# Decoding float64 weights from one copy, with the sign moved by an activation, in an attention and two-layer gated network kernel

## The chip, the cores and the metric

The kernel runs on one core of one Trainium2 chip. The metric is the device time of one execution in microseconds (us). Three runs of the kernel before gave 648.14, 648.49 and 649.67 us, median 648.49 us. One more execution was profiled: it took 648.26 us, of which the trace spans 646.5 us from the first to the last instruction; 1.8 us lie around the span.

The engines are TensorE (PE; PEld is its weight load), VectorE (DVE), ScalarE (ACT), GpSimd (POOL) and SyncE (SP), which here only issues transfers. Each engine works through its own list of instructions in order.

## The reference

The weights `w_in`, `w_out` (first layer) and `w_gate`, `w_val`, `w_out` (second layer) arrive as float64; q, k and v are float32.

```python
k_sum = k.reshape(B, H, nb, block, D).max(axis=3)      # block = 32
v_sum = v.reshape(B, H, nb, block, D).mean(axis=3)
mask_l = np.abs(pos[:, None] - pos[None, :]) < window  # window = 16
scores_s = scale * einsum(q, k_sum) + np.log(block)
scores_all = concat([where(mask_l, scale * q @ k.T, -1e9), scores_s])
a = softmax(scores_all)                                # eps 1e-9 in the sum
x = a @ concat([v, v_sum])                             # 2 x 8 heads, 768 tokens, 64 wide
...
h = x @ w_in                                           # 1536 tokens, 512 -> 2048
x = (h / (1 + np.exp(-1.702 * h))) @ w_out             # 2048 -> 512
gate = 1 / (1 + np.exp(-(x @ w_gate)))                 # 512 -> 1536
return (gate * (x @ w_val)) @ w_out2                   # 1536 -> 512
```

## The kernel before, in words

**Attention.** There are 24 units: two batches, three groups of four query blocks, four pairs of heads. For each unit PE adds a mask and forms the scores (`ps_s`, L560 and L562), DVE takes the negative row maximum (`nm`, L567), ACT the exponentials with their sums (`e`, L575), DVE and POOL normalise (`rs` L582, `rr` L584, `e` L589), PE transposes (`ps_p`, L595), DVE copies (`pt`, L600), PE multiplies by the values (`ps_x`, L610), and the result is split into a rounded part `xH` (ACT, L628) and the rest `xL` (DVE, L631). POOL scales the keys (`kx`, L551), DVE takes maxima of keys (`ks`, L540) and sums of values (`vm`, L523).

**Layers.** Every large product is three matmuls in fp32r on high and low parts (L359 and L131). The first layer works on groups of 256 columns of its 2048 hidden columns and blocks of 512 tokens: `first` forms `ps_h`, gates it (ACT L383, DVE L374, ACT L375, POOL L376), and `second` multiplies by `w_out` into `ps_o`, which DVE adds to `acc` (L439). The first four of these steps are woven into the attention loop as a filler for PE. The second layer does two of its three token blocks with seven products instead of eight, from sums of weight blocks and of token blocks (`combine`, `token_sums`, `pair`).

**Weights.** There are 34 pieces of 128x1024 float64 elements, 1024 KB each. `fetch` issues two transfers for each piece: `raw` (L172), the words as they lie, and `mid` (L174), the same bytes shifted by 16 bits. Both have one buffer; the second piece goes to the buffers of `xH` and `xL` instead. `decode` makes a high part and a low part from them in six DVE and two ACT instructions, all on 128x1024 elements: the upper words as float32 are clamped (L104) and scaled on ACT (L105); the bits of the low part are cut out of `mid` (L108); the upper word is shifted left by 3 and masked (L110), the sign is put back (L112), ACT casts that to fp32r as the high part (L115); the exponent is cut out (L117), and bits times exponent times a constant is the low part (L119). `load` and `load_group` run these steps, one at each `yield`, and fetch the next piece after the first step; `pull(n)` takes n steps at a point of the loop.

**Order.** Transfers on SP stand in the order in which the program writes them. On the other engines the kernel is built with a scheduler that orders instructions by its own estimate of times, so the order of `pull` calls is only one of its inputs. In an engine's list an instruction that waits holds all behind it.

Of the kernel before, what the change touches and what calls it, by code (L numbers as in the profile page):

```python
# [8 lines left out]
F32 = mybir.dt.float32  # L9
F32R = mybir.dt.float32r  # L10
U32 = mybir.dt.uint32
U16 = mybir.dt.uint16
BF16 = mybir.dt.bfloat16
AF = mybir.ActivationFunctionType
ALU = mybir.AluOpType
# [14 lines left out]
def attention_moe_moe2_kernel(ctx: ExitStack, tc: tile.TileContext, ins: dict, out: bass.AP):  # L30
# [23 lines left out]

    const = ctx.enter_context(tc.tile_pool(name="const", bufs=1))
    xp = ctx.enter_context(tc.tile_pool(name="xp", bufs=NTB))
    wraw = ctx.enter_context(tc.tile_pool(name="wraw", bufs=1))
    wtmp = ctx.enter_context(tc.tile_pool(name="wtmp", bufs=1))

    ident = const.tile([P, P], F32, name="ident")  # L60
# [28 lines left out]
    acc_a = ctx.enter_context(tc.tile_pool(name="acc_a", bufs=1))  # L89
    ps_h = ctx.enter_context(tc.tile_pool(name="ps_h", bufs=2, space=PSUM))  # L90

    def decode(raw, mid, hi_out, lo_out):

        n = raw.shape[1] // 2
        head = raw.rearrange("p (n t) -> p n t", t=2)[:, :, 1]
        tail = mid.rearrange("p (n t) -> p n t", t=2)[:, :, 0]
        a, b, c = (wtmp.tile([P, n], U32, tag=f"d{x}", name=f"d{x}") for x in "abc")  # L100
        af, cf = a.bitcast(F32), c.bitcast(F32)
        ts = nc.vector.tensor_scalar

        ts(out=af, in0=head.bitcast(F32), scalar1=F64_MAX, scalar2=-F64_MAX, op0=ALU.min, op1=ALU.max)  # L104
        nc.scalar.activation(af, af, AF.Copy, scale=REBIAS)  # L105
        yield

        ts(out=b, in0=tail, scalar1=0x01FFFFFF, scalar2=None, op0=ALU.bitwise_and)  # L108
        yield
        ts(out=c, in0=a, scalar1=3, scalar2=0x7FFFF000, op0=ALU.logical_shift_left, op1=ALU.bitwise_and)  # L110
        yield
        nc.vector.scalar_tensor_tensor(  # L112
            out=c, in0=a, scalar=0x80000000, in1=c, op0=ALU.bitwise_and, op1=ALU.bitwise_or
        )
# [43 lines left out]
    for layer, g, i in wanted:  # L158
        w = mats[layer][i]
        last = i == len(mats[layer]) - 1  # L160
        src = [rows_of(x, g) if last else cols_of(x, g, n) for x, n in ((w.bitcast(U32), 2), (w.bitcast(U16), 4))]
        pieces.append((f"{layer}_{g}_{i}", *src))

    def fetch():

        if pieces:
            name, src, shifted = pieces.pop(0)
            n, m = src.shape[1], src.shape[2]

            homes = ((xp, "xH"), (xp, "xL")) if name == "1_0_1" else ((wraw, "raw"), (wraw, "mid"))  # L170
            raw, mid = (p.tile([P, n * m], U32, tag=t, name=f"{t}{name}") for p, t in homes)
# [3 lines left out]
            raws.append((raw, mid, (P, n, m // 2)))  # L175

    def load(slots, layer, g, i):
        raw, mid, shape = raws.pop(0)
        hi, lo = (slots.tile(list(shape), F32R, name=f"w{layer}_{g}_{i}{x}") for x in "HL")
        parts = decode(raw, mid, hi.rearrange("p a n -> p (a n)"), lo.rearrange("p a n -> p (a n)"))  # L180
# [283 lines left out]
    with tc.manual_schedule(engines={mybir.EngineType.SP}), ExitStack() as es:  # L464
# [236 lines left out]
        for t in range(-1, NU + LD):  # L701
            now[0] = t

            u = t + 2
            if u < NU and units[u][1] == 0:
                prep_k(units[u][0], units[u][2])
            for part, lag in ORDER:
                if 0 <= t - lag < NU:
                    part(t - lag)
            if 0 <= t < NU - 5:  # L710
                load_q(t + 5, nc.sync)
            if t == -1:
                sum_v(0, 0)
                sum_v(0, 1)
            if t == 0:
                sum_v(0, 2)
                sum_v(0, 3)
                sum_lay(0)
                load_v(0, 1)
                put_v(0, 0)  # L720
                put_v(0, 1)
            if t in (6, 7, 8, 9):
                sum_load(1, t - 6)
            if t in (7, 8, 9, 10):
# [12 lines left out]
            for _ in range(2 if t >= 8 else 1):  # L737
                next(fill, None)
        for _ in fill:
# [107 lines left out]
```

## Time and profile before

| | |
|---|---|
| median of three runs | 648.49 us |
| profiled execution | 648.26 us |
| its span | 646.5 us |
| PE busy | 619.0 us (96%) |
| DVE busy | 487.4 us (75%), 706 instructions |
| ACT busy | 277.1 us (43%) |
| POOL busy | 199.5 us (31%) |
| moved by DMA | 93.96 MB |

The busy shares are averages over a stage with the attention, which lasts to about 146 us, and the two layers behind it. A busy PE is one in which some matmul is in flight; how fast it advances is seen from the starts of its matmuls and from the granted clock. The chain of waits follows the execution back from its last instruction: each piece is the work that released the next.

### The profile page before, as it was taken

Reading aid. Unit: us, or ns where it says so; the run is one execution under the profiler, and the core shown is the slowest. Engines: PE = TensorE matmul, PEld = TensorE weight load, DVE = VectorE, ACT = ScalarE, POOL = GpSimd, SP = SyncE. Lnnn points to the kernel's source line nnn. Section 1 sums busy time; section 2 is a strip of 40 time slices with the busy share of each in tenths; the row PEclk is TensorE's granted clock in tenths of the full one; section 3 lists DMA queues with packets and bytes.
Section 4 is the critical chain, followed back from the end, with each engine's and each line's share of the span. In section 5 each row is a group of like instructions: output and inputs, shape, how many; then the busy total and the mean of one; then the engine's idle time right before and its main releaser. Section 6 shows DMA issues by size and latency. Waiting matters only on the chain.

```text
span 646.5 us, 8331 instructions
## 1 busy us (share of the span) xinstructions
PE 619.0 (96%) x3096; PEld 504.7 (78%) x3098; DVE 487.4 (75%) x706; ACT 277.1 (43%) x548; POOL 199.5 (31%) x164
## 2 busy tenths in 40 slices
PE   7578799999999999999999999999999999999997
PEld 4455588778888888888888888888887888888886
DVE  6799747539999876767657999279689689698434
ACT  3455566745544323332335555453344343343320
POOL 6555567513323322222221222032031030140210
PEclk9768899999999999999999999999999999999999
DMA  9999773207767433330102333333432533430004
GB/s 313 359 370 319 227 245 80 50 1 259 261 241 277 134 131 130 131 130 2 65 2 65 131 131 132 129 112 100 178 131 75 186 131 113 147 130 1 1 33 162
DMA packets 39672, 93.96 MB, mean 145 GB/s; under 512 B 2128, under 2 KB 12624, under 8 KB 39632
## 3 DMA queue, kind: packets, MB, share of 16 engines
q1 hardware_dynamic: 39056, 92.39, 42.2%
q10 hardware_dynamic: 576, 1.05, 0.4%
q8 instruction: 24, 0.39, 0.3%
q14 instruction: 16, 0.13, 0.1%
HBM read 88.71 MB, written 3.15 MB: 142 GB/s over the span
## 4 chain that ended last, share of the span: by engine, by line
PE 85%; DVE 8%; ACT 3%; DMA 2%; issue 1%; POOL 0%; SPq 0%; ACTq 0%; DVEq 0%; POOLq 0%
PE ps_o L359 35%; PE ps_h L359 20%; PE ps_v L131 9%; PE ps_y L131 7%; PE ps_x L131 5%; PE ps_h L131 4%; PE ps_s L562 2%; DMA q<-in_q 1%; PE ps_x L610 1%; DVE dc L112 1%; PE ps_p L595 1%; ACT e L575 1%; DMA vt<-in_vt 1%; DVE dc L110 1%; DVE sg L374 1%
## 5 line engine op out<-in xcount | busy, mean ns | idle before, releaser
L376 POOL TENSOR_TENSOR gl<-sg,gh 128x512 fp32r<-128x512 f32 x84 | 127.7, 1523 | 389.6 <-ACT gh L375 360.5
L439 DVE TENSOR_TENSOR acc<-ps_o,acc 128x512 f32<-128x512 f32 x143 | 96.3, 684 | 37.4 <-PE ps_o L359 37.3
L375 ACT CAST gh<-sg 128x512 fp32r<-128x512 f32 x84 | 52.1, 621 | 90.6 <-DVE sg L374 81.8
L359 PE MATMUL ps_o<-gl,w_1H 128*128 128x512 f32 x192 | 75.9, 395 | 0.7 <-POOL gl L376 0.7
L359 PE MATMUL ps_h<-xL,w_0H 128*128 128x512 f32 x192 | 75.7, 394 | 0.0
L359 PE MATMUL ps_o<-gh,w_1L 128*128 128x512 f32 x192 | 75.2, 398 | 0.5 <-ACT gh L375 0.4
L359 PE MATMUL ps_h<-xH,w_0L 128*128 128x512 f32 x192 | 75.5, 397 | 0.0
L359 PE MATMUL ps_o<-gh,w_1H 128*128 128x512 f32 x192 | 75.4, 393 | 0.0
L359 PE MATMUL ps_h<-xH,w_0H 128*128 128x512 f32 x192 | 75.3, 392 | 0.0
L374 DVE TENSOR_TENSOR sg<-ps_h,sg 128x512 f32<-128x512 f32 x48 | 32.8, 685 | 33.1 <-ACT sg L383 33.0
L359 PE MATMUL ps_o<-w_2H,gl 128*128 128x512 f32 (+1 forms) x146 | 56.3, 388 | 0.5 <-DVE acc L439 0.4
L359 PE MATMUL ps_o<-w_2L,gh 128*128 128x512 f32 (+1 forms) x146 | 56.4, 386 | 0.0
L359 PE MATMUL ps_o<-w_2H,gh 128*128 128x512 f32 (+1 forms) x146 | 56.4, 386 | 0.0
L383 ACT ACTIVATE sg<-ps_h 128x512 f32<-128x512 f32 x48 | 28.3, 595 | 55.7 <-PE ps_h L359 55.7
L105 ACT ACTIVATE da<-da 128x1024 f32<-128x1024 f32 x34 | 36.1, 1061 | 27.9 <-DVE da L104 27.9
L359 PEld LDWEIGHTS ps_o<-gh,w_1L 128*128 128x128 f32 x192 | 36.2, 189 | 11.4 <-ACT gh L375 3.7
L112 DVE SCALAR_TENSOR_TENSOR dc<-da,dc 128x1024 uint32<-128x1024 uint32 x34 | 44.4, 1307 | 0.6
L575 ACT ACTIVATE e<-ps_s,nm 128x128 f32<-128x128 f32 x96 | 34.0, 369 | 23.6 <-PE ps_p L595 11.8
L359 PEld LDWEIGHTS ps_o<-gl,w_1H 128*128 128x128 f32 x192 | 36.4, 190 | 8.3 <-POOL gl L376 1.0
L359 PEld LDWEIGHTS ps_h<-xH,w_0L 128*128 128x128 f32 x192 | 36.1, 189 | 8.1 <-ACT xH L628 0.6
L359 PEld LDWEIGHTS ps_h<-xL,w_0H 128*128 128x128 f32 x192 | 36.2, 189 | 7.6
L359 PEld LDWEIGHTS ps_h<-xH,w_0H 128*128 128x128 f32 x192 | 36.3, 189 | 7.5
(157 smaller groups left out, 1293.8 us busy)
## 6 DMA issues: line engine op xcount, KB each, us to landing
raw<-in_moe_w_out SPq DMA_DIRECT2D x13, 1024.0 KB, 4.9
mid<-in_moe_w_out SPq DMA_DIRECT2D x13, 1023.5 KB, 6.4
raw<-in_moe_w_in SPq DMA_DIRECT2D x8, 1024.0 KB, 5.4
mid<-in_moe_w_in SPq DMA_DIRECT2D x8, 1023.0 KB, 7.7
raw<-in_moe_w_gate SPq DMA_DIRECT2D x6, 1024.0 KB, 5.2
raw<-in_moe_w_val SPq DMA_DIRECT2D x6, 1024.0 KB, 5.1
mid<-in_moe_w_gate SPq DMA_DIRECT2D x6, 1023.0 KB, 7.3
mid<-in_moe_w_val SPq DMA_DIRECT2D x6, 1023.0 KB, 7.0
```

The costliest lines, as they stand in the source:

```text
L105: nc.scalar.activation(af, af, AF.Copy, scale=REBIAS)
L110: ts(out=c, in0=a, scalar1=3, scalar2=0x7FFFF000, op0=ALU.logical_shift_left, op1=ALU.bitwise_and)
L112: nc.vector.scalar_tensor_tensor(out=c, in0=a, scalar=0x80000000, in1=c, op0=ALU.bitwise_and, op1=ALU.bitwise_or)
L131: nc.tensor.matmul(ps, lhsT=a[x][:, kk, :], rhs=b[y][:, kk, :], start=start and i == 0, stop=i == n - 1, skip_group_check=True,)
L359: nc.tensor.matmul(ps, lhsT=a, rhs=b, start=i == 0, stop=i == n - 1)
L374: nc.vector.tensor_tensor(out=sg, in0=val, in1=sg, op=ALU.mult)
L375: nc.scalar.copy(gh, sg)
L376: nc.gpsimd.tensor_tensor(out=gl, in0=sg, in1=gh, op=ALU.subtract)
L383: nc.scalar.activation(sg, ps, AF.Sigmoid, scale=1.702 if layer == 1 else 1.0)
L439: nc.vector.tensor_tensor(out=a[:, m, :], in0=ps, in1=a[:, m, :], op=ALU.add)
L562: nc.tensor.matmul(ps[:, j, :], lhsT=t[:, j, :], rhs=kt[:, j, :], start=False, stop=j == G - 1)
L575: nc.scalar.activation(e[:, j, :], s[:, j, :], AF.Exp, bias=nm[:, j:j + 1], accum_out=sm[:, j:j + 1])
```

## The change

`decode` reads one copy of the piece. The clamp stays. The scaling on ACT is now a Prelu with a negative slope (`alpha`), which multiplies negative elements by a further -2^32: they become positive, and their sign is kept as bit 28 of the word. DVE shifts the lower words right by 29 (L105 in the new file), then one instruction shifts the scaled upper word left by 3, which takes bit 28 to the sign, and joins the three bits from the lower word (L107). ACT casts this float32 to fp32r as the high part (L110), and DVE subtracts the high part from it as the low part (L112). So a decode has four DVE and two ACT instructions, and the last DVE instruction reads what the cast wrote. `fetch` issues one transfer, `raw` has two buffers, the tile `dc` and all `mid` tiles are gone, and for t below 6 the attention loop takes one step of decoding at a time, where it took two.

```diff
-    wraw = ctx.enter_context(tc.tile_pool(name="wraw", bufs=1))
+    wraw = ctx.enter_context(tc.tile_pool(name="wraw", bufs=2))
...
-    def decode(raw, mid, hi_out, lo_out):
+    def decode(raw, hi_out, lo_out):
         n = raw.shape[1] // 2
-        head = raw.rearrange("p (n t) -> p n t", t=2)[:, :, 1]
-        tail = mid.rearrange("p (n t) -> p n t", t=2)[:, :, 0]
...
+        words = raw.rearrange("p (n t) -> p n t", t=2)
+        tail, head = words[:, :, 0], words[:, :, 1]
...
         ts(out=af, in0=head.bitcast(F32), scalar1=F64_MAX, scalar2=-F64_MAX, op0=ALU.min, op1=ALU.max)
-        nc.scalar.activation(af, af, AF.Copy, scale=REBIAS)
+        nc.scalar.activation(af, af, AF.Prelu, scale=REBIAS, alpha=-2.0 ** 32)
         yield
-        ts(out=b, in0=tail, scalar1=0x01FFFFFF, scalar2=None, op0=ALU.bitwise_and)
-        yield
-        ts(out=c, in0=a, scalar1=3, scalar2=0x7FFFF000, op0=ALU.logical_shift_left, op1=ALU.bitwise_and)
+        ts(out=b, in0=tail, scalar1=29, scalar2=None, op0=ALU.logical_shift_right)
         yield
         nc.vector.scalar_tensor_tensor(
-            out=c, in0=a, scalar=0x80000000, in1=c, op0=ALU.bitwise_and, op1=ALU.bitwise_or
+            out=a, in0=a, scalar=3, in1=b, op0=ALU.logical_shift_left, op1=ALU.bitwise_or
         )
-        nc.scalar.copy(hi_out, cf)
+        nc.scalar.copy(hi_out, af)
         yield
-        ts(out=a, in0=c, scalar1=0xFF800000, scalar2=None, op0=ALU.bitwise_and)
-        yield
-        nc.vector.scalar_tensor_tensor(out=lo_out, in0=b, scalar=2.0 ** -36, in1=af, op0=ALU.mult, op1=ALU.mult)
+        nc.vector.tensor_tensor(out=lo_out, in0=af, in1=hi_out, op=ALU.subtract)
         yield
...
             nc.sync.dma_start(out=raw.rearrange("p (a n) -> p a n", a=n), in_=src)
-            to = mid.bitcast(U16).rearrange("p (a n) -> p a n", a=n)
-            nc.sync.dma_start(out=to[:, :, 0:2 * m - 1], in_=shifted[:, :, 1:])
...
             if t >= 1:
-                pull(2)
+                pull(1 if t < 6 else 2)
```

Three places in the built programs. On DVE, from the first decode (piece `0_0`) to its low part, in the kernel before; `da`, `db`, `dc` are the decode's work tiles, the other names are those of the attention:

```order
L104 TENSOR_SCALAR da<-raw_0_0_152 128x1024
L582 TENSOR_SCALAR rs<-sm 128x4
L584 RECIPROCAL rr<-rs 128x4
L582 TENSOR_SCALAR rs<-sm 128x4
L584 RECIPROCAL rr<-rs 128x4
L108 TENSOR_SCALAR db<-mid_0_0_153 128x1024
L110 TENSOR_SCALAR dc<-da 128x1024
L112 SCALAR_TENSOR_TENSOR dc<-da,dc 128x1024
L117 TENSOR_SCALAR da<-dc 128x1024
L119 SCALAR_TENSOR_TENSOR w_0_0L<-db,da 128x1024
```

The same place on DVE with the change:

```order
L102 TENSOR_SCALAR da<-raw_0_0_152 128x1024
L105 TENSOR_SCALAR db<-raw_0_0_152 128x1024
L573 TENSOR_SCALAR rs<-sm 128x4
L575 RECIPROCAL rr<-rs 128x4
L573 TENSOR_SCALAR rs<-sm 128x4
L575 RECIPROCAL rr<-rs 128x4
L107 SCALAR_TENSOR_TENSOR da<-da,db 128x1024
L558 TENSOR_REDUCE nm<-ps_s 128x4
L105 TENSOR_SCALAR db<-xH_0_1_154 128x1024
L112 TENSOR_TENSOR w_0_0L<-da,w_0_0H 128x1024
```

The instruction that makes `db` has moved ahead of the two `rs`, the two that made `dc` and the masked `da` are gone, and an attention maximum and the first instruction on the second piece stand between the joining and the subtraction.

On ACT, from the first scaling on, before:

```order
L105 ACTIVATE da<-da 128x1024
L115 CAST w_0_0H<-dc 128x1024
L105 ACTIVATE da<-da 128x1024
L115 CAST w_0_1H<-dc 128x1024
L575 ACTIVATE e,sm<-ps_s,nm 128x128 x4
L628 CAST xH_327<-ps_x 128x256
```

The same place on ACT with the change:

```order
L103 ACTIVATE da<-da 128x1024
L110 CAST w_0_0H<-da 128x1024
L566 ACTIVATE e,sm<-ps_s,nm 128x128 x4
L619 CAST xH_317<-ps_x 128x256
L103 ACTIVATE da<-da 128x1024
L566 ACTIVATE e,sm<-ps_s,nm 128x128 x4
L110 CAST w_0_1H<-da 128x1024
```

The exponentials and the `xH` of an attention unit now stand between the two decodes, and four exponentials ahead of the second cast.

On SP, from the first piece's transfer on, before:

```order
L172 DMA raw_0_0_152<-in_moe_w_in 128x4x512
L174 DMA mid_0_0_153<-in_moe_w_in 128x4x1023
L172 DMA xH_0_1_156<-in_moe_w_out 128x2x1024
L174 DMA xL_0_1_157<-in_moe_w_out 128x2x2047
L493 DMA q_215<-in_q 128x512
L505 DMA vwin<-in_v 96x4x512
```

The same place on SP with the change:

```order
L165 DMA raw_0_0_152<-in_moe_w_in 128x4x512
L165 DMA xH_0_1_154<-in_moe_w_out 128x2x1024
L484 DMA q_211<-in_q 128x512
L496 DMA vwin<-in_v 96x4x512
```

Two transfers of about 1 MB each no longer stand ahead of the next query tile.

## Rows read from the trace of the kernel before

**Rows 1.** Page part 2: busy tenths in 40 slices of 16.2 us.
```profile
PE   7578799999999999999999999999999999999997
DVE  6799747539999876767657999279689689698434
DMA  9999773207767433330102333333432533430004
```

**Rows 2.** Chain of waits, whole span: start us, us, what.
```profile
174.20 5.44 PE ps_h L359 x24
```

**Rows 3.** Stretches: start:end, length, PE PEld DVE ACT POOL busy us, clock, DMA, GB/s.
```profile
20.00:40.00 20.00, 11.09 (x73) 8.44 (x72) 17.10 (x27) 9.73 (x33) 9.68 (x11) 0.67 1.05 346
40.00:60.00 20.00, 15.07 (x137) 11.89 (x134) 19.07 (x38) 12.00 (x47) 13.38 (x12) 0.84 1.01 337
160.00:200.00 40.00, 40.00 (x178) 33.14 (x177) 38.92 (x49) 19.43 (x28) 11.84 (x7) 1.00 0.73 256
```

**Rows 4.** Chain of waits from 25 to 58 us.
```profile
26.45 1.46 DVE dc L110
...
27.93 1.23 DVE dc L112
...
29.19 0.70 DVE da L117
...
32.99 0.70 DVE dc L110
...
35.54 0.61 DVE da L117
...
42.74 1.45 DVE dc L110
...
46.85 0.64 DVE da L117
...
53.66 0.58 DVE dc L110
...
57.65 0.63 PE ps_p L595 x4
```

**Rows 5.** Timeline of DVE: start us, us, line, out<-in [idle before <-releaser].
```profile
26.37 1.53 DVE L110 TENSOR_SCALAR dc<-da 128x1024 uint32<-128x1024 uint32 x1
...
32.99 0.69 DVE L110 TENSOR_SCALAR dc<-da 128x1024 uint32<-128x1024 uint32 x1 [0.21 <-ACT da L105]
...
58.67 1.00 DVE L117 TENSOR_SCALAR da<-dc 128x1024 uint32<-128x1024 uint32 x1
...
67.62 0.68 DVE L110 TENSOR_SCALAR dc<-da 128x1024 uint32<-128x1024 uint32 x1
68.21 0.42 DVE L631 TENSOR_TENSOR xL<-ps_x,xH 128x256 fp32r<-128x256 f32 x1
```

**Rows 6.** Timeline of POOL at the two long instructions of L110.
```profile
26.04 1.30 POOL L589 TENSOR_TENSOR e<-e,rr 128x512 f32<-128x512 f32 x1 [0.48 <-DVE rr L584]
...
42.34 1.30 POOL L589 TENSOR_TENSOR e<-e,rr 128x512 f32<-128x512 f32 x1 [0.59 <-DVE rr L584]
```

**Rows 7.** Timeline of ACT at the first decode.
```profile
25.02 1.09 ACT L105 ACTIVATE da<-da 128x1024 f32<-128x1024 f32 x1
29.18 1.05 ACT L115 CAST w_0H<-dc 128x1024 fp32r<-128x1024 f32 x1 [3.08 <-DVE dc L112]
```

**Rows 8.** Groups by line on DVE: xcount | busy us, mean ns | idle before <-releaser.
```profile
L117 DVE TENSOR_SCALAR da<-dc 128x1024 uint32<-128x1024 uint32 x34 | 31.9, 938 | 0.5
...
L110 DVE TENSOR_SCALAR dc<-da 128x1024 uint32<-128x1024 uint32 x34 | 27.2, 799 | 2.6 <-ACT da L105 2.6
...
L119 DVE SCALAR_TENSOR_TENSOR w_0L<-db,da 128x1024 fp32r<-128x1024 uint32 x14 | 17.0, 1217 | 0.2
...
L230 DVE TENSOR_TENSOR sL<-ws,sH 128x1024 fp32r<-128x1024 f32 x12 | 15.7, 1310 | 2.0 <-ACT sH L229 2.0
```

**Rows 9.** Timeline of PE: the scores that wait for a query tile.
```profile
29.22 1.20 PE L562 MATMUL ps_s<-kx,q 128*128 128x128 f32 x4 [3.63 <-DMA q<-in_q]
```

More of the change, by code (lines that the diff above doesn't have):

```diff
@@ L11 @@
 U32 = mybir.dt.uint32
-U16 = mybir.dt.uint16
 BF16 = mybir.dt.bfloat16
@@ L90, in attention_moe_moe2_kernel @@
     ps_h = ctx.enter_context(tc.tile_pool(name="ps_h", bufs=2, space=PSUM))
-    def decode(raw, mid, hi_out, lo_out):
+    def decode(raw, hi_out, lo_out):
         n = raw.shape[1] // 2
-        head = raw.rearrange("p (n t) -> p n t", t=2)[:, :, 1]
-        tail = mid.rearrange("p (n t) -> p n t", t=2)[:, :, 0]
-        a, b, c = (wtmp.tile([P, n], U32, tag=f"d{x}", name=f"d{x}") for x in "abc")
-        af, cf = a.bitcast(F32), c.bitcast(F32)
+        words = raw.rearrange("p (n t) -> p n t", t=2)
+        tail, head = words[:, :, 0], words[:, :, 1]
+        a, b = (wtmp.tile([P, n], U32, tag=f"d{x}", name=f"d{x}") for x in "ab")
+        af = a.bitcast(F32)
         ts = nc.vector.tensor_scalar
         ts(out=af, in0=head.bitcast(F32), scalar1=F64_MAX, scalar2=-F64_MAX, op0=ALU.min, op1=ALU.max)
-        nc.scalar.activation(af, af, AF.Copy, scale=REBIAS)
+        nc.scalar.activation(af, af, AF.Prelu, scale=REBIAS, alpha=-2.0 ** 32)
         yield
-        ts(out=b, in0=tail, scalar1=0x01FFFFFF, scalar2=None, op0=ALU.bitwise_and)
-        yield
-        ts(out=c, in0=a, scalar1=3, scalar2=0x7FFFF000, op0=ALU.logical_shift_left, op1=ALU.bitwise_and)
+        ts(out=b, in0=tail, scalar1=29, scalar2=None, op0=ALU.logical_shift_right)
         yield
         nc.vector.scalar_tensor_tensor(
-            out=c, in0=a, scalar=0x80000000, in1=c, op0=ALU.bitwise_and, op1=ALU.bitwise_or
+            out=a, in0=a, scalar=3, in1=b, op0=ALU.logical_shift_left, op1=ALU.bitwise_or
         )
-        nc.scalar.copy(hi_out, cf)
+        nc.scalar.copy(hi_out, af)
         yield
-        ts(out=a, in0=c, scalar1=0xFF800000, scalar2=None, op0=ALU.bitwise_and)
-        yield
-        nc.vector.scalar_tensor_tensor(out=lo_out, in0=b, scalar=2.0 ** -36, in1=af, op0=ALU.mult, op1=ALU.mult)
+        nc.vector.tensor_tensor(out=lo_out, in0=af, in1=hi_out, op=ALU.subtract)
         yield
@@ L160, in attention_moe_moe2_kernel @@
         last = i == len(mats[layer]) - 1
-        src = [rows_of(x, g) if last else cols_of(x, g, n) for x, n in ((w.bitcast(U32), 2), (w.bitcast(U16), 4))]
-        pieces.append((f"{layer}_{g}_{i}", *src))
+        x = w.bitcast(U32)
+        pieces.append((f"{layer}_{g}_{i}", rows_of(x, g) if last else cols_of(x, g, 2)))
     def fetch():
         if pieces:
-            name, src, shifted = pieces.pop(0)
+            name, src = pieces.pop(0)
             n, m = src.shape[1], src.shape[2]
-            homes = ((xp, "xH"), (xp, "xL")) if name == "1_0_1" else ((wraw, "raw"), (wraw, "mid"))
-            raw, mid = (p.tile([P, n * m], U32, tag=t, name=f"{t}{name}") for p, t in homes)
+            home, tag = (xp, "xH") if name == "1_0_1" else (wraw, "raw")
+            raw = home.tile([P, n * m], U32, tag=tag, name=f"{tag}{name}")
             nc.sync.dma_start(out=raw.rearrange("p (a n) -> p a n", a=n), in_=src)
-            to = mid.bitcast(U16).rearrange("p (a n) -> p a n", a=n)
-            nc.sync.dma_start(out=to[:, :, 0:2 * m - 1], in_=shifted[:, :, 1:])
-            raws.append((raw, mid, (P, n, m // 2)))
+            raws.append((raw, (P, n, m // 2)))
     def load(slots, layer, g, i):
-        raw, mid, shape = raws.pop(0)
+        raw, shape = raws.pop(0)
         hi, lo = (slots.tile(list(shape), F32R, name=f"w{layer}_{g}_{i}{x}") for x in "HL")
-        parts = decode(raw, mid, hi.rearrange("p a n -> p (a n)"), lo.rearrange("p a n -> p (a n)"))
+        parts = decode(raw, hi.rearrange("p a n -> p (a n)"), lo.rearrange("p a n -> p (a n)"))
         for step, _ in enumerate(parts):
```

## The prediction

> **What bounds the kernel now.** I read the 40 slices first [rows 1]. PE is at 9 from the ninth slice to the last but one, so from about 130 us on, and nearly so from 80 us, it is never without a matmul; before that its digits are 5 to 8. Whether a busy PE also advances at its full pace is told by the whole chain of waits [rows 2]: 24 matmuls of 512 columns took 5.44 us, 0.227 us each; such pieces follow one another from there almost to the end. A weight decode that gets faster there is worth nothing in itself, since PE waits for nothing of it. What can be won lies in the first 80 us.
>
> Then the stretches [rows 3]. From 20 to 40 us DVE is busy for 17.10 of 20 us, from 40 to 60 us for 19.07; the DMA share is 1.05 and 1.01 at 346 and 337 GB/s, while PE is busy for 11.09 and 15.07 at a mean clock of 0.67 and 0.84, and ACT for 9.73 and 12.00. Two resources are full, DVE and the transfers, and the change takes work from both. Which of them sets the time is read from the chain of waits of this stretch [rows 4]: from 26.45 to 57.65 us it lies on DVE, with a few links of ACT and POOL between, and at 57.65 it goes over to PE. The transfers ran full beside it, but no transfer is a link of the chain there. So the early stage is a queue on DVE, in which the instructions of four decodes stand between those of the attention units, and PE starts its steady work when the units have come through.
>
> **The change part by part.**
>
> *Two DVE instructions fewer in each decode.* L110 and L117 go. Seven of them are links of the chain before it turns to PE [rows 4]: L110 with 1.46, 0.70, 1.45 and 0.58, together 4.19 us, and L117 with 0.70, 0.61 and 0.64, together 1.95 us; in all 6.14 us. Taken away from an in-order queue that is the chain, that is what they give back, if nothing else grows.
>
> *But two of them were long for a reason that stays.* L110 took 1.53 us at 26.37 and 0.69 us at 32.99 [rows 5]; at 26.37, and again at 42.7, POOL was in its L589 of 1.30 us, which had just been released by the reciprocal on DVE [rows 6]. The POOL instruction stays, and another DVE instruction will stand beside it. If that one then loses as much, the two long links count only with the 0.64 us that is the mean of the two short ones: 6.14 - (1.46 + 1.45 - 2 x 0.64) = 4.51 us. I take the middle of 4.51 and 6.14, 5.32 us, because the next instruction there, the joining, is of the kind of L112, which kept 1.23 us in the chain [rows 4], yet now starts earlier in POOL's 1.30 us.
> The Trainium skill, page "SBUF — State Buffer", section "Who interferes with whom", says that VectorE and GpSimd share one pair of ports, held for a whole instruction by whichever starts first, and that a VectorE instruction with two SBUF inputs is caught by it too, not only one in a two-port mode. By that rule the joining inherits the loss, and the sum below would end at 642.6 us; by the rows taken as they stand (6.14) at 640.9 us. The trace agrees in that the same instruction takes 0.69 us alone and 1.53 us beside POOL; it does not show which instruction pays next.
>
> *Moved at the first decode.* The instruction that makes `db` goes ahead of the two `rs`. It is a shift of the kind of L110, 0.58 to 0.70 us when alone. What then holds the joining is the scaling on ACT, which stands behind the exponentials and ended at 25.02 + 1.09 = 26.11 us [rows 7]. So the joining can start at about 26.13 where L112 started at 27.93 [rows 4], 1.80 us earlier, of which 1.46 are counted with L110: 0.34 us more. The Prelu itself is not in the trace. Nearest are the Copy with scale (1.09) and the cast (1.05) of the same size [rows 7]; I take the same. From below nothing speaks for less; from above, a Prelu of twice the time would put four times 1.05 us on the chain.
>
> *Kept or swapped.* The clamp stays, the cut of `mid` becomes a shift of the same size, the last instruction (L119, 1.217 us) becomes a subtraction, which elsewhere in the kernel has 1.310 us at the same size [rows 8], nearly all of the difference in a few long ones. I count both at nothing; the ends are 0 and 4 x 0.09 = 0.4 us.
>
> *A new wait.* The low part now needs the cast, so DVE stands still if the cast is late, and behind it stand the attention's maxima, copies and `xL`, for which PE waits. A cast takes 1.05 us. In the new order a maximum and the first instruction of the second piece stand between the joining and the subtraction at the first decode, about 1.2 us, and the cast is next on ACT behind the scaling: hidden. At the second, ACT has four exponentials ahead of the cast, and DVE six small and middle instructions ahead of the subtraction: hidden by about as much. I take 0 and keep 4 x 1.05 = 4.2 us as the other end. What is left of ACT there, 9.73 and 12.00 us busy in 20 [rows 3], leaves room.
>
> *After the chain has gone to PE.* L117 of the fourth decode, 1.00 us at 58.67, and L110 of the fifth, 0.68 us at 67.62, stand in front of the last `xL` of the first 512 tokens at 68.21 [rows 5], which PE needs for its first layer. PE is only just ahead of DVE there, so I take half of the 1.68: 0.84 us.
>
> *Half of the weight transfers.* At 346 GB/s [rows 3] the two shifted copies ahead of the next query tile are 2.05 MB or 5.9 us of a full queue. PE waited 3.63 us for such a tile at 29.22 [rows 9], while the chain was on DVE. So the tile comes earlier, and PE with it, but DVE takes its maximum no sooner than the queue lets it. I count it at nothing; the other end is 3.63 us. The second raw buffer and the single step of `pull` for t below 6 bring attention instructions ahead of decodes, which moves work within the same queue.
>
> *The layers.* 29 decodes lie behind the attention, beside a full PE: 0 us.
>
> Sum: 5.32 + 0.34 + 0.84 = 6.50 us. The profiled execution took 648.26 us, so 641.76 us, 641.8. It lies 0.23 us below the median of the three runs, which changes nothing here.
>
> **The rivals.**
>
> *More comes back: the transfers count in full.* If DVE stops being the queue because it is relieved, PE's query waits become the next link and are gone too. Then all ten instructions up to 68 us count, with the means of their groups, 5 x (0.799 + 0.938) = 8.69 us [rows 8], with 0.34 and 3.63: 12.66 us, or 635.6 us. For it speaks the DMA share above 1.0 [rows 3]; against it that no transfer is a link from 26 to 58 us.
>
> *Little comes back: the casts are seen.* With the lower value for the removed links and four casts in full, 4.51 + 0.34 - 4.20 = 0.65 us: 647.6 us; with one or two of them seen, 644 to 646.5 us. Against it stands the new order.
>
> *Slower: the wait for the cast, in the layers.* There DVE adds up `ps_o` and gates `ps_h` in order; a subtraction that waits for a cast which itself stands behind a Sigmoid waiting for PE holds all that, and PE runs out of banks. 29 decodes with one cast of 1.05 us each in PE's time would be 30.5 us, and 648.26 + 30.5 - 6.5 = 672 us; it decides from 6.5 / 29 = 0.22 us of PE for each decode. The place is 160 to 200 us, where DVE is busy for 38.92 of 40 us [rows 3]. Against it: the kernel has this very pattern already, a cast on ACT and a subtraction behind it, in L230, twelve times, and DVE stood still for it 2.0 us in all [rows 8] while PE's digits stay at 9 [rows 1]; and five decodes of that stretch give up 5 x (0.799 + 0.938) = 8.7 us of DVE, more than five casts of 1.05.
>
> *It doesn't do what it says.* A Prelu that needed its own function table would add a load around each of 34 scalings. The built list of ACT holds eight table loads with the change, as before, so I give this no chance of its own.
>
> **How the numbers follow.** A difference of 0.3%, 1.95 us, is about what a measurement of this kernel can tell from no change. The forecast, 638.5 to 644.5 us, gets 0.60; more comes back 0.15; little comes back 0.18, of which 0.11 still ends more than 1.95 us below 648.5; slower 0.07, of which 0.05 by more than 1.95 us. So faster 0.60 + 0.15 + 0.11 = 0.86, the same 0.07 + 0.02 = 0.09, slower 0.05. The range runs from 637.0, which leaves out the half of the first rival that is nearest to its end, to 645.8, which leaves out the two cases at the slow end beyond one or two casts.
>
> **What would show it.** L110 and L117 have no successor, and DVE's busy time falls by about 31.9 + 27.2 = 59 us; the early digits of DVE and DMA fall. In the chain from 26 us on the DVE links are shorter and the change to PE comes 5 to 7 us earlier, at 50 to 53 us; from 160 us on the chain is PE at 0.227 us as before. New idle time of DVE in front of the subtraction, released by the cast, would be the cost I put at nothing: above about 1 us in all before 60 us it takes its part from the sum. The prediction is wrong if PE shows gaps from 150 us on, if the first PE link behind DVE is not earlier, or if more than 9 us come back.

## The result, and the profile after

The change made the kernel slower. Four runs gave 653.73 to 654.68 us, median 654.59; beside them the kernel before had 648.81 us. The ratio is 1.0085, with a 95% interval of 1.0068 to 1.0103. Timed once more later, the ratio was 1.0060 (1.0043 to 1.0077). All medians here are those of fast runs: one execution of the later run e18, 882.24 us at a granted clock of 0.66, is left out. The profiled execution took 653.73 us, its span is 651.9 us, 5.4 us more than before.

The page's 40 slices, the answer to [rows 1]:

```profile
PE   6686799799999999999999999999999999999997
...
DVE  6798536328897565657557998249579579597424
...
DMA  9977840203443122220002212101411221200004
```

DVE and DMA fell as the change intends (DVE from 487.4 to 435.2 us, transfers from 93.96 to 58.33 MB), but PE's fourth digit (49 to 65 us) is a 6 where it was an 8, and its eighth (114 to 130 us) a 7 where it was a 9. In stretches (columns as in [rows 3]), first the kernel before, then the changed one:

```profile
20.00:160.00 140.00, 121.81 (x913) 96.15 (x915) 100.03 (x182) 79.42 (x245) 73.61 (x71) 0.91 0.64 205
160.00:380.00 220.00, 220.00 (x972) 182.19 (x971) 177.78 (x232) 91.82 (x132) 57.75 (x38) 1.00 0.40 137
```

```profile
20.00:160.00 140.00, 117.27 (x885) 91.66 (x887) 87.24 (x166) 76.54 (x241) 72.94 (x68) 0.93 0.49 150
160.00:380.00 220.00, 220.00 (x972) 182.16 (x971) 153.92 (x199) 90.81 (x133) 58.34 (x40) 1.00 0.21 68
380.00:420.00 40.00, 39.36 (x174) 32.23 (x173) 28.80 (x35) 20.14 (x31) 6.76 (x5) 1.00 0.22 77
```

From 160 to 380 us PE is full in both, so the decodes of that stretch cost nothing. The loss is made before 160 us: PE is busy for 4.5 us less there. A small one of 0.6 us stands between 380 and 420 us (40.00 before).

Where it is made is read from DVE's timeline of the changed kernel. The units' results `xL` of the first 512 tokens are eight; PE needs all of them to end the first layer's first product, and the two `sg` gate that product. `vm` and `ks` here belong to the second batch, whose first `xL`, the thirteenth, ends only at 100.1 us:

```profile
50.09 0.41 DVE L622 TENSOR_TENSOR xL<-ps_x,xH 128x256 fp32r<-128x256 f32 x1
...
52.84 0.95 DVE L514 TENSOR_REDUCE vm<-vt 128x24 f32<-128x768 f32 x1 [2.25 <-DMA vt<-in_vt]
54.16 0.95 DVE L531 TENSOR_REDUCE ks<-k 128x24 f32<-128x768 f32 x1 [0.37 <-DMA k<-in_k]
...
56.76 0.94 DVE L514 TENSOR_REDUCE vm<-vt 128x24 f32<-128x768 f32 x1
...
57.95 0.41 DVE L622 TENSOR_TENSOR xL<-ps_x,xH 128x256 fp32r<-128x256 f32 x1
58.28 0.94 DVE L531 TENSOR_REDUCE ks<-k 128x24 f32<-128x768 f32 x1
...
63.70 0.41 DVE L622 TENSOR_TENSOR xL<-ps_x,xH 128x256 fp32r<-128x256 f32 x1
...
64.63 0.94 DVE L531 TENSOR_REDUCE ks<-k 128x24 f32<-128x768 f32 x1
...
68.28 0.39 DVE L622 TENSOR_TENSOR xL<-ps_x,xH 128x256 fp32r<-128x256 f32 x1
...
71.70 0.69 DVE L365 TENSOR_TENSOR sg<-ps_h,sg 128x512 f32<-128x512 f32 x1 [0.43 <-ACT sg L374]
74.10 0.95 DVE L531 TENSOR_REDUCE ks<-k 128x24 f32<-128x768 f32 x1 [1.71 <-DMA k<-in_k]
74.97 0.68 DVE L365 TENSOR_TENSOR sg<-ps_h,sg 128x512 f32<-128x512 f32 x1
```

The fifth `xL` starts at 50.09 us and ends at 50.5; before, it ended at 57.8, as the chain turned to PE [rows 4]. So 7.3 us were won by then. DVE's timeline of the kernel before:

```profile
57.42 0.41 DVE L631 TENSOR_TENSOR xL<-ps_x,xH 128x256 fp32r<-128x256 f32 x1
```

The eighth starts at 68.28 us, where it had started at 68.21 [rows 5]: all of it is gone again within three units. In between stand `vm` and `ks` of the second batch, some of them waiting for their own transfers. The chain of waits shows the worst of them:

```profile
45.82 8.32 DMA k<-in_k
...
66.08 8.00 DMA k<-in_k
...
74.10 0.95 DVE ks L531
75.06 0.61 DVE sg L365
...
75.71 0.79 PE ps_o L350
76.50 1.05 PE ps_x L601 x16
```

A `k` of 400 KB is in flight for 8 us; a `ks` on DVE waits for it; the second gate `sg` stands behind that `ks`; PE waits 2.11 us for the gate. Then PE goes on more slowly: the sixteen `ps_x` took 1.12 us there, and 0.69 us at 69.84 us, where PE had not stood still before them. In PE's timeline:

```profile
69.84 0.69 PE L601 MATMUL ps_x<-pt,vwin 128*64 128x64 f32 x16
...
75.71 0.79 PE L350 MATMUL ps_o<-gh,w_1L 128*128 128x512 f32 x1 [2.11 <-DVE sg L365]
76.43 1.12 PE L601 MATMUL ps_x<-pt,vwin 128*64 128x64 f32 x16
```

From 60 to 80 us the granted clock is 0.88 in the mean: a part of this stretch ran at the lower of its two levels (1.2 and 2.4 GHz). Two more gaps lie at 122 to 125 us, 1.59 us in front of `ps_p` and 1.77 us in front of `ps_o`:

```profile
124.85 0.73 PE L350 MATMUL ps_o<-gh,w_1L 128*128 128x512 f32 x2 [1.77 <-ACT gh L366]
```

They are of another kind: no `ks` or `vm` stands in front of them. On ACT, between the `sg` and the cast `gh` for which this `ps_o` waits, stand a load of a function table (1.28 us at 121.49) and four exponentials of an attention unit. The faster runs e7, e10 and e17 below have no gap of over 0.8 us on PE between 80 and 140 us.

### The profile page after: what moved, and what is told of

The parts are those of the page before. It is cut to its first block, busy times and chain, and to the rows that moved or that the text cites. A ratio compares the mean times of both kernels' runs of the same rounds, so it can differ in the third digit from the quotient of the medians.

```text
span 651.9 us, 8226 instructions
## 1 busy us (share of the span) xinstructions
PE 619.1 (95%) x3097; PEld 503.4 (77%) x3098; DVE 435.2 (67%) x638; ACT 275.8 (42%) x548; POOL 194.0 (30%) x164
## 2 busy tenths in 40 slices
DMA packets 25303, 58.33 MB, mean 89 GB/s; under 512 B 1584, under 2 KB 1840, under 8 KB 25264
## 4 chain that ended last, share of the span: by engine, by line
PE 80%; DVE 8%; DMA 6%; ACT 2%; issue 2%; POOL 1%; SPq 0%; ACTq 0%; DVEq 0%; POOLq 0%
PE ps_o L350 34%; PE ps_h L350 19%; PE ps_v L124 8%; PE ps_y L124 6%; PE ps_x L124 5%; PE ps_h L124 4%; DMA k<-in_k 4%; PE ps_s L553 2%; PE ps_x L601 2%; DMA vwin<-vs 1%; DVE wf L206 1%; DVE ws L215 1%; DMA q<-in_q 1%; PE ps_p L586 1%; POOL kx L542 1%
## 5 line engine op out<-in xcount | busy, mean ns | idle before, releaser
L367 POOL TENSOR_TENSOR gl<-sg,gh 128x512 fp32r<-128x512 f32 x84 | 119.3, 1423 | 410.9 <-ACT gh L366 388.7
L107 DVE SCALAR_TENSOR_TENSOR da<-da,db 128x1024 uint32<-128x1024 uint32 x34 | 44.1, 1296 | 13.3 <-ACT da L103 13.0
L103 ACT ACTIVATE da<-da 128x1024 f32<-128x1024 f32 x34 | 36.1, 1061 | 31.0 <-DVE da L102 30.9
L350 PEld LDWEIGHTS ps_o<-gh,w_1H 128*128 128x128 f32 x192 | 36.4, 190 | 7.4
```

The costliest lines, as they stand in the source:

```text
L103: nc.scalar.activation(af, af, AF.Prelu, scale=REBIAS, alpha=-2.0 ** 32)
L107: nc.vector.scalar_tensor_tensor(out=a, in0=a, scalar=3, in1=b, op0=ALU.logical_shift_left, op1=ALU.bitwise_or)
L350: nc.tensor.matmul(ps, lhsT=a, rhs=b, start=i == 0, stop=i == n - 1)
L367: nc.gpsimd.tensor_tensor(out=gl, in0=sg, in1=gh, op=ALU.subtract)
```

## The experiments

The theories at the outset: A, DVE's freed time goes to `ks` and `vm` of the second batch, whose transfers come late behind the load of `vwin`; B, the single step delays the first weights; C, the second raw tile lets weight transfers push others back; D, the wait for the cast in each decode. After the first runs A was split: the place in DVE's queue, or the transfers.

DVE's list is in order, so what stands ahead of the eighth `xL` can be counted in it: instructions of the second batch, `vm` / `ks` / `nm`. "Tiles" are raw tiles, "steps" those that `pull` takes in the first six iterations. All ratios are to the kernel before, run on the same chip.

| run | decode | tiles, steps | ahead of the 8th `xL` | us | ratio (95%) |
|---|---|---|---|---|---|
| before | old | 1, 2 | 3 / 1 / 0 | 648.5 to 649.2 | |
| the change | new | 2, 1 | 4 / 3 / 2 | 654.59 | 1.0085 |
| again (e16) | new | 2, 1 | 4 / 3 / 2 | 652.80 | 1.0060 |
| e1 | new | 2, 2 | 4 / 3 / 2 | 649.65 | 1.0001 (0.9987 to 1.0015) |
| e2 | new | 1, 1 | 4 / 3 / 2 | 650.92 | 1.0032 (1.0018 to 1.0046) |
| e7 | new | 1, 2 | 2 / 0 / 0 | 640.47 | 0.9862 (0.9842 to 0.9881) |
| again (e15) | new | 1, 2 | 2 / 0 / 0 | 641.76 | 0.9885 (0.9868 to 0.9903) |
| e9, early loads | new | 1, 2 | 4 / 3 / 1 | 647.77 | 0.9991 (0.9978 to 1.0003) |
| e10, tied | new | 2, 1 | 2 / 0 / 0 | 640.62 | 0.9870 (0.9854 to 0.9885) |
| e17, tied, early vt | new | 2, 1 | 2 / 0 / 0 | 642.95 | 0.9914 (0.9896 to 0.9931) |
| e13, only vm tied | new | 2, 1 | 3 / 2 / 1 | 646.12 | 0.9963 (0.9951 to 0.9976) |
| e14, only ks tied | new | 2, 1 | 4 / 0 / 0 | 650.03 | 1.0021 (1.0003 to 1.0038) |
| e12, tied | new | 1, 2 | 2 / 0 / 0 | 645.16 | 0.9945 (0.9932 to 0.9958) |
| e18, tied | new | 2, 2 | 2 / 0 / 0 | 642.66 | 0.9906 (0.9878 to 0.9934) |
| e4, late vwin | new | 2, 1 | 4 / 4 / 3 | 649.37 | 0.9995 (0.9980 to 1.0009) |
| e8, late vwin | new | 2, 2 | 4 / 4 / 2 | 652.20 | 1.0042 (1.0026 to 1.0058) |
| e3 | old | 1, 1 | 3 / 1 / 0 | 652.80 | 1.0064 (1.0047 to 1.0081) |
| e5, one transfer | old | 1, 2 | 4 / 2 / 1 | 652.02 | 1.0045 (1.0029 to 1.0061) |
| e6, two instructions less | old | 1, 2 | 3 / 1 / 0 | 647.26 | 0.9972 (0.9959 to 0.9986) |
| e11, tied | old | 1, 2 | 2 / 0 / 0 | 651.74 | 1.0050 (1.0038 to 1.0062) |

The counts say nothing of ACT's list. There each turn from the exponentials to the `sg` of the gate or back has a table load, 1.28 us each in the traces. The kernel before, the change and most runs have eight of them; e3, e12, e13, e14 and e18 have ten, e9 and e11 twelve. So these seven runs differ from the others by more than the counts.

**Undoing one side edit at a time (e1, e2, e3).** e1 and e2 start from the changed kernel, e3 from the kernel before:

```diff
-                pull(1 if t < 6 else 2)      # e1
+                pull(2)
-    ... name="wraw", bufs=2                  # e2
+    ... name="wraw", bufs=1
-                pull(2)                      # e3
+                pull(1 if t < 6 else 2)
```

e1: 

> The changed kernel with two steps of the weight decodes in every iteration of the attention loop, as before, in place of one in the first six. Theory A (the time that VectorE was given is spent on copies of the second batch, ks and vm, whose transfers come late behind the load of vwin): the edit does not touch those transfers; 652.5 to 656.5 us, the eighth xL of the first 512 tokens ends at 67 to 70 us as with the change (68.7). Theory B (the single step puts attention work ahead of the decodes and so delays the first weights): 642 to 649 us, matmul 120 of the first layer at or before 120.6 us (kernel before) in place of 124.8. Theory C (the second raw tile lets weight transfers push others back) and theory D (VectorE waits for the cast in each decode): no change, 653.5 to 655.5 us.

e2: 

> The changed kernel with one raw tile in place of two. Theory A (ks and vm of the second batch wait for transfers behind vwin): about the same, 652.5 to 656.5 us. Theory C (the second raw tile lets weight transfers push the transfers of k and vt back): 642 to 649 us, and the transfer of k_0 that took 8.3 us from issue to landing takes under 5 us. Theories B (single step) and D (wait for the cast): no change, 653.5 to 655.5 us.

e3: 

> The kernel before with one step of the weight decodes in the first six iterations of the attention loop, as in the change, and nothing else changed. Theory B (the single step is what costs): 653 to 656 us. Theories A, C and D: the time of before, 647.5 to 650 us, or up to 2 us less, since the attention units come before the decodes.

e1 and e2 took 2 to 5 us back and brought no gain over the kernel before; B for e1 and C for e2 had expected 642 to 649, the other theories no change, so all missed. Neither edit alone is the whole cause. e3 came out near what B expected (653 to 656), for a reason that the change with its two raw tiles does not have: with one raw tile and one step the next piece is fetched later, and DVE stood still for it, with everything behind it:

```profile
61.79 0.69 DVE L104 TENSOR_SCALAR da<-raw 128x1024 f32<-128x1024 f32 x1 [4.47 <-DMA raw<-in_moe_w_out]
```

**Moving the transfers that stand in the way (e4, e8).** In the changed kernel, up to 110 us, SP waited 24.1 us for PE in front of the loads of `vwin`, with `k` and `vt` queued behind.

```diff
-            if t % HP == HP - 1 and HP < t < NU - HP:
-                c = t // HP + 1
+            if t % HP == 1 and HP + 1 < t < NU:
+                c = t // HP
```

e4: 

> The changed kernel with the loads of vwin and their put (load_v, put_v) issued two iterations of the attention loop later, so that k, vt and q of the next units do not stand behind them on SP's queue, where the load of vwin waits for ps_x of TensorE. Theory A (those late transfers hold ks and vm on VectorE, and VectorE holds xL and sg): 643 to 649 us, SP's waits for ps_x at the load of vwin fall from 24.1 us to under 12, the longest wait for a transfer in front of ks falls from 1.71 us to under 0.5, and matmul 120 of the first layer is at most at 121.5 us in place of 124.8. Theories B (single step), C (second raw tile) and D (wait for the cast): 653 to 656 us.

e8 (with `pull(2)` as well): 

> The changed kernel with both edits that gave some 5 us each: two steps of the decodes in every iteration, and the loads of vwin two iterations later. If they remove two different waits: 643 to 646 us. If both remove the same wait (the eighth xL and the second sg of the first 512 tokens at 74 to 75 us): 648 to 650 us. If the order of VectorE's queue is simply sensitive to any such shift, without a cause in common: anywhere from 645 to 655 us.

e4 took back 3 to 5 us, but not as expected: its eighth `xL` ended at 70.8 us, later than with the change, since its DVE list had all four `ks` ahead. All theories missed its time, A by 0.4 us. e8 is slower than either edit alone, as only the last of its three cases allowed. With e4 the wait on SP fell to 7.2 us without bringing the gain back, so this wait is not the cause as a whole.

**The decode alone (e7), and its two halves (e5, e6).** e7 is the changed kernel with one raw tile and `pull(2)`. e5 keeps the old decode but reads the low bits from `raw`; e6 keeps both transfers but leaves out L110 and L117. Both therefore compute with other weights and serve for timing alone.

```diff
-    ... name="wraw", bufs=2                  # e7
+    ... name="wraw", bufs=1
-                pull(1 if t < 6 else 2)      # e7
+                pull(2)
-        tail = mid.rearrange(...)[:, :, 0]   # e5, from before; the transfer of mid goes too
+        tail = raw.rearrange(...)[:, :, 0]
-        ts(out=c, in0=a, scalar1=3, ...)     # e6, from before: L110 (L112 then takes a)
-        ts(out=a, in0=c, scalar1=0xFF800000, ...)     # and L117
```

e7: 

> The new decode and its one transfer alone: the changed kernel with two steps of the decodes in every iteration and with one raw tile, both as before. If the sum of the prediction held for the decode and only the two side edits spoiled it: 641 to 644 us. If the transfers of q, vt and k become the next link (theory A, after the chain of the run with two steps in every iteration, which has a vt of 8.97 us as a link at 46 us): 647 to 650 us. If the second raw tile is what the one step needs and two steps do not: 649 to 652 us, slower than with two tiles (649.65).

e5: 

> The kernel before, its decode of six VectorE instructions kept, with one transfer for each weight piece in place of two; the low bits are read from the first copy, so the low part of the weights is another one. By the prediction (halved transfers count nothing while the chain lies on VectorE): 647.5 to 649.5 us; by its other end, PE's wait of 3.63 us for q gone: 645 us. Theory A (what comes back is decided by the transfers of q, vt and k): 644 to 646 us.

e6: 

> The kernel before with its two transfers for each piece, but without the two VectorE instructions that the change removes (the shift ahead of the joining and the cut of the exponent); the weights' high and low parts are other ones. By the prediction's term for them alone: 642.4 to 644 us (5.3 to 6.1 us less). Theory A (transfers, which are as many as before, become the link as soon as VectorE is relieved): 646.5 to 649 us.

e7 gained 8.7 us, and 6.9 us when run again: the sum of the prediction, 6.50, comes near to that in size. Its DVE queue has more of the second batch behind the eighth `xL`, with one `vm` and one `ks` less ahead than the kernel before:

```profile
63.70 0.41 DVE L622 TENSOR_TENSOR xL<-ps_x,xH 128x256 fp32r<-128x256 f32 x1
64.35 0.95 DVE L514 TENSOR_REDUCE vm<-vt 128x24 f32<-128x768 f32 x1 [0.25 <-DMA vt<-in_vt]
65.36 0.95 DVE L531 TENSOR_REDUCE ks<-k 128x24 f32<-128x768 f32 x1
...
69.04 0.68 DVE L365 TENSOR_TENSOR sg<-ps_h,sg 128x512 f32<-128x512 f32 x1
```

The eighth `xL` starts 4.6 us earlier than with the change, the second `sg` 5.9 us earlier, and PE in the same stretches, with the clock, is

```profile
20.00:160.00 140.00, 124.70 (x941) 98.20 (x941) 96.07 (x172) 82.51 (x251) 76.55 (x72) 0.96 0.51 150
```

that is 7.4 us more busy than with the change, at a higher clock. Its `ks` wait for late transfers too (1.49 us at 74.79), but none of the instructions that the first 512 tokens' first product needs is behind them. The halves do not add up: two instructions less gain 1.9 us (e6, as theory A expected, with the same counts as before), half the transfers alone lose 2.9 (e5, outside all that was expected), and the new decode, which has both, gains 7 to 9.

**Order or transfers (e9, e10, e11, e12).** e9 takes e7 and issues the loads and sums of the second batch two iterations earlier. e10 keeps both side edits and holds the second batch back by a data dependence: the tiles that `vm` and `ks` go into are cleared by multiplying an `xL` by zero. e11 and e12 put this tie into the kernel before and into e7. With the tie the sums also stand one iteration later in the program, and the key maxima behind the other parts of a unit.

```diff
+        def after_x(out, u):
+            nc.vector.tensor_scalar(out=out, in0=x_slice(xL, u).bitcast(F32)[:, 0:W0],
+                                    scalar1=0.0, scalar2=None, op0=ALU.mult)
...
-                nc.vector.memset(vpart[b], 0.0)
+            if b == 1:
+                after_x(vpart[b][:, hp, :], hp + 5)
...
-            nc.vector.memset(ks, 0.0)
+                after_x(ks, hp + 7)          # for b == 1
```

```diff
-            if t in (6, 7, 8, 9):            # e9; sum_v, sum_lay and load_k likewise
-                sum_load(1, t - 6)
+            if t in (4, 5, 6, 7):
+                sum_load(1, t - 4)
```

e9: 

> The version of 640.5 us (new decode, one raw tile, two steps per iteration) with the loads of vt and k of the second batch and its block sums issued two iterations of the attention loop earlier. In its DVE queue four vm, three ks and a maximum of the second batch then stand ahead of the eighth xL, where the version of 640.5 us has two vm and no ks and the changed kernel four vm, three ks and two maxima. Order theory (what stands ahead of the last xL of the first 512 tokens, waiting for late transfers, is the whole loss; the raw tile and the steps act only through it): 649 to 654 us, the eighth xL at 67 us or later in place of 64.1. Transfer theory (the second raw tile itself costs, by weight transfers that push k, vt and q back): 640 to 643 us.

e10: 

> The changed kernel with both side edits kept (two raw tiles, one step in the first six iterations), but the clearing of vm and ks of the second batch reads the xL of a unit (times zero), so that they cannot stand ahead of it: two vm and no ks ahead of the eighth xL, as in the version of 640.5 us. Order theory: 639 to 644 us, the eighth xL at 63 to 65 us. Transfer theory and the theory that the single step delays the weights: 650 to 655 us.

e11: 

> The kernel before with the same tie: two vm and no ks ahead of the eighth xL in place of three and one, the old decode and its two transfers. If the gain of the new decode is its own, as the prediction's sum has it: 645 to 648.5 us (at most two instructions of 0.95 us and a wait less ahead of the eighth xL). If the decode's gain was only a better order by chance: 639 to 643 us.

e12: 

> The version of 640.5 us with the tie: the same counts ahead of the eighth xL (two vm, no ks), one vm less ahead of the second sg, and eight small VectorE instructions in place of five clearings. Order theory: 638.5 to 642 us. If the tie itself costs (the vs of the second batch comes later, and with it vwin and the first unit of that batch): 643 us or more.

e10 answers it: with two tiles and one step as in the change, seven instructions of the second batch moved behind the eighth `xL` in DVE's list, and 654.59 becomes 640.62 us. (The clamp, the shift and the joining of the fifth decode moved behind it too; e17 below has them ahead again.) The tie in its DVE timeline, behind the sixth and the eighth `xL`:

```profile
55.76 0.42 DVE L633 TENSOR_TENSOR xL<-ps_x,xH 128x256 fp32r<-128x256 f32 x1
56.21 0.18 DVE L506 TENSOR_SCALAR vm<-xL 128x32 f32<-128x32 f32 x1
...
63.12 0.41 DVE L633 TENSOR_TENSOR xL<-ps_x,xH 128x256 fp32r<-128x256 f32 x1
63.56 0.18 DVE L506 TENSOR_SCALAR ks<-xL 128x32 f32<-128x32 f32 x1
```

With that the chain of waits turns to PE at 52.85 us, where the prediction had placed the turn (50 to 53), 4.8 us earlier than in the kernel before (57.65):

```profile
52.85 1.12 PE ps_x L612 x16
```

e9, with one tile, two steps and early loads, lost 6.0 to 7.3 us of the gain, less than the order theory expected and more than the transfer theory did. It points the same way but does not settle it, for it has twelve table loads, and its second `sg` waited 1.74 us for ACT, behind a load, and not behind a `ks`.

e11 missed both its ranges; in e12 the order theory missed, and the other case came, that the tie itself costs. The old decode with the good counts is 3 us slower than the kernel before, and the tie costs e7 3.4 to 4.7 us though the counts are the same. Tied against tied the new decode is 651.74 - 645.16 = 6.6 us better, but with ten loads against twelve, so that e11 neither excludes that a part of e7's gain is order nor gives the decode's own worth. Where e12 loses can be read: from 100 to 120 us PE is busy for 17.71 us at a clock of 0.91, in e7 for 19.54 at 1.00. Exponentials stand between its two `sg` there, and with them two more loads, and PE waits. One line of ACT and one of PE:

```profile
113.99 1.28 ACT L374 ACT_TABLE_LOAD   x1
...
116.44 0.80 PE L350 MATMUL ps_o<-gh,w_1L 128*128 128x512 f32 x1 [2.04 <-ACT gh L366]
```

That the loads make up the whole of e12's loss no run shows. Among the runs with eight loads, those with 2 / 0 / 0 lie at 640.5 to 643.0 us, all others at 647.3 us or more.

**Which of them, and when the transfers go (e13, e14, e17, e18).** e13 and e14 have only one of the two `after_x` calls (e13 with `hp + 4`); e17 is e10 with four `vt` tiles, so that the transfers need not wait for the tied `vm`; e18 is e10 with `pull(2)`; e15 and e16 repeat e7 and the change.

```diff
-            t = vp.tile([P, S], F32, tag="vt", bufs=2, ...)   # e17
+            t = vp.tile([P, S], F32, tag="vt", bufs=4, ...)
```

e13: 

> The changed kernel with only the vm of the second batch tied to an xL each, the ks free: three vm, two ks and one maximum of the second batch stand ahead of the eighth xL, where the changed kernel has four, three and two, and the fully tied one two, none and none. If each such instruction costs by itself: 646 to 650 us. If it is the ks and the maxima behind them that cost: 647 to 653 us. If it is the vm: 643 to 648 us.

e14: 

> The changed kernel with only the ks of the second batch tied to an xL each, the vm free: four vm, no ks and no maximum of the second batch ahead of the eighth xL. If the ks and the maxima behind them cost (a ks waits for a k that lies behind the load of vwin, a maximum takes PE's scores of the second batch forward): 640 to 644 us. If the vm cost as much: 645 to 650 us.

e17: 

> The tied version of 640.6 us with four vt tiles in place of two: VectorE's queue up to the eighth xL is the same (two vm, no ks ahead of it), SP's list is the same, but no vt has to wait for a vm, so that the third and fourth vt and the k behind them are issued at about 45 to 47 us as in the changed kernel, in place of 57 and 62 us. If the place in VectorE's queue carries the loss: 639 to 644 us. If the early transfers carry it (they push q and the raw weights back): 648 to 654 us.

e18: 

> The tied version of 640.6 us with two steps of the decodes in every iteration in place of one in the first six; two raw tiles. If, with the queue held, neither side edit matters: 639.5 to 642 us. If the one step and the two tiles are worth the 4.5 us that lie between this version and the tied one with one tile and two steps (645.2): 643 to 646 us.

e15: 

> The version of 640.5 us (new decode, one raw tile, two steps) once more, beside the changed kernel on one chip: 639.5 to 642 us.

e16: 

> The changed kernel once more, beside the version of 640.5 us on one chip: 653 to 655.5 us.

I had expected the `ks` to carry more. With only the `ks` held (e14), 2.8 to 4.6 us came back, against 6.7 to 8.5 us with only the `vm` held (e13); both have ten loads, so the shares are rough. In e14 the `vm`, ahead of the sixth `xL`, still waited:

```profile
55.62 0.95 DVE L519 TENSOR_REDUCE vm<-vt 128x24 f32<-128x768 f32 x1 [2.39 <-DMA vt<-in_vt]
...
60.42 0.42 DVE L630 TENSOR_TENSOR xL<-ps_x,xH 128x256 fp32r<-128x256 f32 x1
```

e17 tells the queue from the transfers. SP's timeline from 44 us, the third `vt` of the second batch and a `k`, in e17 and then in e10 (in the change they go at 44.91 and 45.82):

```profile
46.48 0.90 SPq L512 DMA_DIRECT2D vt<-in_vt  x1
47.43 0.62 SPq L477 DMA_DIRECT2D k<-in_k  x1
```

```profile
57.40 0.33 SPq L512 DMA_DIRECT2D vt<-in_vt  x1
57.77 0.43 SPq L477 DMA_DIRECT2D k<-in_k  x1
```

With the transfers nearly as early as in the change and the second batch held, the time is 642.95 us, as the queue theory expected. So 9.9 to 11.6 us of the loss go with the place of these instructions in DVE's queue. At most the 2.3 us between e17 and e10 go with the transfers and with the clamp, the shift and the joining of the fifth decode, which in e17 stand ahead of the eighth `xL` again. A raw piece came late there, and DVE waited for it:

```profile
61.84 0.69 DVE L102 TENSOR_SCALAR da<-raw 128x1024 f32<-128x1024 f32 x1 [3.11 <-DMA raw<-in_moe_w_in]
```

e18, at 642.66 us, fell between its two ranges. It is 2.0 us above e10, but the intervals of their ratios overlap and e18 has ten loads, so that it does not show what the step costs with the queue held. Of the repeats, e15 came as expected and e16 0.2 us below its range.

## Why the prediction was wrong, step by step

- **The failed step** is the last sentence on the halved transfers: that the second raw buffer and the single step bring attention instructions ahead of decodes, "which moves work within the same queue", priced at nothing. Either edit costs 8 to 10 us on top of the new decode (e1 and e2 against e7 and e15), both together 11 to 14. What the runs showed in its place: with these edits nine instructions of the second batch stand ahead of the eighth `xL`, with the decode alone two; held back to two with both edits kept, 9.9 to 14.0 us come back (e17, e10). I counted which instructions went and looked at the order up to the decodes, not at what came to stand ahead of the eighth `xL` and the second `sg`, for which PE waits. What took the place of the freed time in this queue is work of the second batch, some of which waited for transfers of 8 us.
- **The two removed instructions, the start of the joining, the half after the chain's change** (5.32 + 0.34 + 0.84): the sum 6.50 comes near the 6.9 to 8.7 us of e7 and e15 as a number. That it is made up of these terms is not shown: the instructions alone gave 1.9 (e6), and e7 also has half the transfers and a `vm` and a `ks` less ahead of the eighth `xL`. The agreement is in part luck.
- **The halved transfers at nothing**: wrong when alone (+2.9 us, e5, whose list puts six instructions of the second batch and a maximum ahead of the eighth `xL`, in place of four).
- **The long links beside POOL**: right that the loss stays and passes on. In e7 the joining took 1.20 us at 27.00, ahead of POOL's `e`, and 2.07 at 52.44, just behind one:

```profile
27.00 1.20 DVE L107 SCALAR_TENSOR_TENSOR da<-da,db 128x1024 uint32<-128x1024 uint32 x1
...
52.44 2.07 DVE L107 SCALAR_TENSOR_TENSOR da<-da,db 128x1024 uint32<-128x1024 uint32 x1
```

```profile
27.25 1.84 POOL L580 TENSOR_TENSOR e<-e,rr 128x512 f32<-128x512 f32 x1 [0.48 <-PE ps_s L553]
...
52.39 1.04 POOL L580 TENSOR_TENSOR e<-e,rr 128x512 f32<-128x512 f32 x1 [3.95 <-DVE rr L575]
```

  The Trainium skill, page "SBUF — State Buffer", section "Who interferes with whom", says that VectorE and GpSimd lock one shared pair of ports against each other. These rows agree: the one that starts second pays, DVE 0.87 us at 52.44, POOL 0.80 at 27.25.
- **The Prelu**: right. 34 took 1061 ns each, against 1.09 us for the Copy in [rows 7], and the trace after has eight table loads, as before. The groups by line of the changed kernel, ACT and then DVE, with the subtraction's wait for the cast at the end of its rows:

```profile
L103 ACT ACTIVATE da<-da 128x1024 f32<-128x1024 f32 x34 | 36.1, 1061 | 31.0 <-DVE da L102 30.9
```

```profile
L112 DVE TENSOR_TENSOR w_1L<-da,w_1H 128x1024 fp32r<-128x1024 f32 x14 | 18.6, 1332 | 10.7 <-ACT w_1H L110 10.7
L112 DVE TENSOR_TENSOR w_0L<-da,w_0H 128x1024 fp32r<-128x1024 f32 x14 | 18.0, 1286 | 1.3 <-ACT w_0H L110 1.3
```

- **The wait for the cast**: right where it counted. Before 60 us DVE does not stand still for it; over the whole span it did so for 10.7 and 1.3 us in these two groups, nearly all of it beside a full PE. The rival that it makes the layers slower is refuted: from 160 to 380 us PE was busy for 220.00 of 220 us. What the layers do lose is 0.6 us near 404 us.
- **The signs I named**: DVE's busy time fell by 52.2 us, not 59. The change of the chain to PE did not come 5 to 7 us earlier: from 45.82 us on the chain of the changed kernel lies on two transfers of `k` and on DVE, and it turns to PE only at 75.71, 18 us later than before. By this the prediction had named itself wrong. That DVE was through with the fifth `xL` 7.3 us earlier looks like the sign but is not it. The gaps on PE lay at 73 to 76 and at 122 to 125 us; the second lies outside the first 80 us, to which the prediction had confined what counts, and before the 150 us from which it watched for gaps.
- **The reading of [rows 1]**: the 9s of PE begin with the sixth slice (81 us), not the ninth; nothing else hangs on it.
- **"Slower"** had 0.07 and one mechanism, the cast. The real one, a refilled queue, was no rival.

The version with the decode alone, one tile and two steps (e7), beats both kernels: 640.47 and 641.76 us; so does e10.

## What to carry to other kernels

Time freed in an in-order queue can be refilled with other work when the order is built anew, and if that is work of a later stage whose transfer is late, as here, the freed time becomes a wait in front of the work that mattered. So after a change that relieves an engine, list what now stands ahead of the instruction that the bound engine waits for, to the end of the stage, and price each with its wait; and do it for every engine, as the table loads on ACT show, which came and went with edits to other engines' work. And a side edit to buffers or to the pace of a loop is a change of order: give it a price of its own or leave it out.

## What the runs showed of the hardware

The two pieces of `k` (400 KB each) in the chain of the changed kernel took 8.32 and 8.00 us from issue to landing, and one in e7 11.02 us from 70.39 us on. The mean share of the DMA engines was 0.81 from 40 to 60 us and 0.74 from 60 to 80 in the changed kernel, and 1.03 from 60 to 80 in e7. Why a piece takes that long at a mean share below 1 is not shown. A gap of 2.11 us on PE was followed by sixteen matmuls in 1.12 us that took 0.69 before it, so that this gap cost more than its length. A load of ACT's function table took 1.28 us, and how many there are, eight, ten or twelve, differed between these runs with the order of ACT's list. Open stay the order of the runs above 646 us among themselves, and how much of e12's loss the two more loads make.
